# Weights converted in pieces of 1024 columns, a third query buffer and fewer filling products in a kernel of attention and a two-layer network

## The chip, the cores and the metric

The kernel runs on one core of a Trainium2 chip. The metric is the device time of one execution in microseconds. Before the change three runs gave 907.27, 908.99 and 909.57, a median of 908.99.

A core has five engines with a queue of instructions each, taken in order: TensorE (PE; its weight loads are shown as PEld), VectorE (DVE), ScalarE (ACT), GpSimd (POOL) and SyncE (SP), which here issues nearly all transfers. Sixteen DMA engines carry them out.

## The reference, cut to what matters

Attention of 8 batches, 8 heads, 576 positions and head dimension 64, within a window (heads 0 to 3: the last 32 positions; heads 4 to 7: every fourth of the last 128), then a two-layer network over 4608 tokens with d_model 512 and d_ff 2048:

```python
scores = scale * np.matmul(q, k.transpose(0, 1, 3, 2))
scores = np.where(masks[None], scores, -1000000000.0)
attn = np.exp(scores - np.max(scores, axis=-1, keepdims=True))
attn = attn / (np.sum(attn, axis=-1, keepdims=True) + 1e-09)
x = np.matmul(attn, v)          # then heads side by side: 4608 x 512
...
h = x @ w_in
sp = np.maximum(h, 0.0) + np.log1p(np.exp(-np.abs(h)))
g = h * erf(sp)
return (g @ w_out).astype(np.float32)
```

The two weight matrices arrive as numbers of 64 bits; the kernel turns each into a pair of 32-bit parts on the chip.

## The kernel before, in words

**Attention.** The work is cut into 72 units of 4 blocks of 64 queries. `scores` (32 small products, L214), `mask_max` on DVE (L225, four calls), `exponents` on ACT (L235, four calls), `normalize` (a reciprocal on DVE, a product on POOL, L247 and L248), `transposes` on PE (L253), `turned`, which copies their result out (L257), `values` (32 small products, L272), and `rows` on ACT (L314), which gathers the results as rows of x^T. When all units of a pair of heads are there, `finish` splits the row tile into a high and a low part (`part_hi` on ACT, L319; `part_lo` on DVE, L325), for the first tokens, or stores it (`store_x`, L344).

**The opening.** The first `FIRST` = 14 units are visited by `first_visit(n)`, with no large product beside them: visit n does the scores of unit n and the values of unit n - 3 (`LAG`), with `busy` filling products (L354) in between, on PE. Query tiles `qkz` are two, used in turn; `load_qk(n + 2)` follows the scores of n in SP's queue. Eight filling products stand ahead of the first visit; visits 0 to 2 have 6 each, the later ones 2 and 2. Visits 1 to 9 (`EARLY`) also convert weights, and copy the transposed probabilities by ACT; the others by DVE.

**The weights.** `prep` is a list of 32 pieces of 128 x 512 numbers (16 of w_in, 16 of w_out), sorted by the step that needs them. A piece is loaded by `load_w` (L421) into one of three places `dbl0` to `dbl2` of 512 KB. `prep_act` does two things on ACT: it copies a finished piece as the high part (L436), and takes the absolute value of the next loaded piece (L441). `prep_dve` subtracts for an earlier piece's low part (L450), and for the current one does a shift (L454) and two merges of bit fields (L455, L456); then the place is free and the next load into it is issued. One call handles each of three pieces at a different stage, one call per visit and afterwards one per half-step x. Intermediate values lie in a tile `w` with four buffers.

**The main loop.** x counts half-steps; step t = x // 2 handles 256 of the 2048 columns of d_ff for a chunk of 512 tokens, and x takes 128 of them. `mm1` (L518, 12 products; from the fourth chunk on `mm1_fast`, L639) fills the PSUM tile `h`; `take` (L660) copies it out by DVE and frees it; `argument` (Softplus, L664) and `table` (Erf, L667) are ACT's, `gate` (L674, L677, L678) is DVE's, `mm2` (L692, 12 products) runs two steps later. Units of attention are put in by `visits()`: one in each of x = 0 to 6, then at 9, 11 and 14, then two at a time by the list `PACE`. `weights(x)` stands ahead of `mm1` for x < 4, and behind the gate after that. `exponents` follow at even x. The order is written by hand, and each engine's queue has the order of the code.

**The saved sums.** The first chunk is done half, then the second whole, then the rest of the first. At x = 11 (`SAVED`) `save` copies the four partial sums out of PSUM and stores them: two go to the halves of `dbl2`, one to a tile of its own, one to `pz[1]`. Loads asked for at x = 11 are held until those stores are issued, and place 2 is not reloaded in x = 8 to 11; `load_w(2)` comes directly behind `save`. Later `dbl0` to `dbl2`, the tile `plain` and `w` serve other things: sums of weights (`sum_whole`, L528), fetched tokens, differences (`right_less`) and outputs (`store`).

Of the kernel before, what the change touches and what calls it, by code (L numbers as in the profile page):

```python
# [13 lines left out]
I32 = mybir.dt.int32  # L14
# [53 lines left out]
EARLY = 9  # L68
# [68 lines left out]
def attn_moe_kernel(ctx: ExitStack, tc: tile.TileContext, qk, v, masks, eye, w_in, w_out, out):  # L137
# [70 lines left out]
    def scores(u):  # L208
        i = u % 2
        for s in range(SPU):  # L210
            at, (p, r) = QW + key_start(u, s), divmod(s, SIDE)
            for h in range(2):
                hs = slice(h * D, (h + 1) * D)
                nc.tensor.matmul(sps[h][r * STRIP:(r + 1) * STRIP, i, p, :], qkz[i][hs, s * STRIP:(s + 1) * STRIP],  # L214
                                 qkz[i][hs, at:at + KEYS], start=True, stop=True,
# [133 lines left out]
    idle = plain.bitcast(BF16)[:, 0:TOK]  # L349
# [48 lines left out]

    def doubles(i):
        return io.tile([P, TOK, 2], I32, name=f"dbl{i}", bufs=1)  # L400
# [16 lines left out]
    def load_w(i):  # L417
        if prep:
            _, src, hi, lo = prep.pop(0)
            d = doubles(i)  # L420
# [3 lines left out]
    def like(w, part):  # L424

        return w.rearrange("p (a j n) -> p a j n", a=2, j=PAIR) if len(part.shape) == 4 else w

    calls = [0]

    def prep_act():  # L430


        calls[0] += 1
        if made:
            w, hi, lo = made.popleft()
            nc.scalar.copy(out=hi, in_=like(w, hi))  # L436
            rest.append((calls[0], w, hi, lo))
        if staged:
            i, d, hi, lo = staged.popleft()
            w = io.tile([P, TOK], F32, name="w", bufs=4)  # L440
            nc.scalar.activation(out=w, in_=d[:, :, 1].bitcast(F32), func=AF.Abs, scale=REBASE)  # L441
# [481 lines left out]
```

## Time and profile before

| | |
|---|---|
| Median of three runs | 908.99 us |
| Profiled execution, and its span | 909.89 us, 907.8 us |
| PE, PEld busy in the span | 886.3 us (98%), 754.2 us (83%) |
| DVE, ACT, POOL busy | 669.4 us (74%), 600.5 us (66%), 76.9 us (8%) |
| DMA moved | 188.89 MB, mean 208 GB/s |
| First product of the large matrices | 50.81 us |

The page gives busy times of the engines over the span, and groups of instructions by line. Views of the trace give the same for stretches of time, the waits (who waited for whom), the chain of work that ended last, and the instructions in order of time. An instruction's row has its start and its duration in microseconds, engine, line, operation, the tile written and the tiles read, the shape, and in brackets how long the engine had been idle and what released it. `dbl` is the place of a loaded piece, `w` its intermediate value, `win`, `wout_hi` and `wout_lo` the converted weights. A product counts as busy until its last result is out, so that consecutive ones overlap.

### The profile page before, as it was taken

The numbers are of one execution on the slowest core, as the hardware profiler recorded it, in microseconds if no ns is written. First come the engines' busy times: TensorE is split into PE (matmuls) and PEld (weight loads), VectorE is DVE, ScalarE is ACT, GpSimd is POOL, SyncE is SP. The second block draws the span as 40 slices with busy tenths as digits, with TensorE's granted clock in tenths as the row PEclk, the third lists the DMA queues.
The fourth block names the chain that finished last, engine by engine and source line by source line (L and its number), as shares of the span: only waits on it lengthen the run. The fifth ranks groups of instructions, "written<-read, shape, count | busy, mean of one in ns | idle before, by whom it ended". The sixth has DMA issues, their size and how long they took to land.

```text
span 907.8 us, 22886 instructions
## 1 busy us (share of the span) xinstructions
PE 886.3 (98%) x9142; PEld 754.2 (83%) x9142; DVE 669.4 (74%) x1703; ACT 600.5 (66%) x1266; POOL 76.9 (8%) x97
## 2 busy tenths in 40 slices
PE   7799999999999999999999999999999999999998
PEld 3467777888887888889988988888988999999996
DVE  5888878876788888667876777678666866776555
ACT  6889879876678687666776676669654644545442
POOL 2312100000011100000100000001000000000000
PEclk9899999999999999999999999999999999999999
DMA  8874444432459688777658765877566546656521
GB/s 276 278 258 151 123 164 130 155 109 94 156 190 330 216 304 296 245 274 233 217 212 284 264 211 189 290 262 256 179 242 230 181 149 230 235 176 205 200 82 47
DMA packets 69450, 188.89 MB, mean 208 GB/s; under 512 B 9184, under 2 KB 17632, under 8 KB 63200
## 3 DMA queue, kind: packets, MB, share of 16 engines
q1 hardware_dynamic: 69056, 186.91, 60.5%
q8 instruction: 72, 1.18, 0.5%
q10 hardware_dynamic: 288, 0.52, 0.1%
q14 instruction: 34, 0.28, 0.1%
HBM read 153.85 MB, written 33.55 MB: 206 GB/s over the span
## 4 chain that ended last, share of the span: by engine, by line
PE 85%; DVE 7%; ACT 3%; DMA 3%; issue 1%; POOL 0%; SPq 0%; DVEq 0%; POOLq 0%; ACTq 0%
PE acc L692 40%; PE h L639 15%; PE tx L639 12%; PE h L518 10%; PE sp L272 3%; PE sp L214 3%; DMA dbl<-in_w_in_dram 2%; PE sp L253 1%; ACT prob L235 1%; PE h L354 1%; DVE s L674 1%; DVE hc L660 1%; PE acc L272 1%; DVE ghi L677 0%; DVE w L455 0%
## 5 line engine op out<-in xcount | busy, mean ns | idle before, releaser
L692 PE MATMUL acc<-wout_hi,ghi 128*128 128x512 f32 x576 | 228.4, 397 | 0.4 <-DVE ghi L677 0.2
L692 PE MATMUL acc<-wout_lo,ghi 128*128 128x512 f32 x576 | 225.6, 392 | 0.0
L664 ACT ACTIVATE s<-hc 128x1024 f32<-128x1024 f32 x72 | 76.5, 1062 | 188.5 <-DVE hc L653 171.1
L692 PE MATMUL acc<-wout_hi,glo 128*128 128x512 f32 x576 | 159.0, 389 | 0.0
L692 PEld LDWEIGHTS acc<-wout_hi,glo 128*128 128x128 f32 x576 | 108.1, 188 | 22.8
L692 PEld LDWEIGHTS acc<-wout_hi,ghi 128*128 128x128 f32 x576 | 108.5, 188 | 20.6 <-DVE ghi L677 0.8
L692 PEld LDWEIGHTS acc<-wout_lo,ghi 128*128 128x128 f32 x576 | 108.6, 189 | 19.6
L248 POOL TENSOR_TENSOR prob<-prob,rinv 128x256 f32<-128x256 f32 x72 | 69.2, 971 | 536.0 <-DVE ssum L246 313.7
L678 DVE TENSOR_TENSOR glo<-s,ghi 128x512 fp32r<-128x512 f32 x144 | 100.0, 694 | 5.5 <-PE acc L692 0.5
L235 ACT ACTIVATE prob<-prob,nmax 128x64 f32<-128x64 f32 x288 | 96.4, 339 | 8.3 <-DVE nmax L225 7.8
L674 DVE TENSOR_TENSOR s<-hc,s 128x1024 f32<-128x1024 f32 x72 | 92.9, 1290 | 9.1 <-ACT s L667 9.0
L639 PE MATMUL h<-win 128*128 128x256 f32 x720 | 98.1, 283 | 0.0
L518 PE MATMUL h<-x,win 128*128 128x512 f32 x384 | 96.6, 393 | 1.5 <-DVE hc L660 1.5
L664 ACT ACT_TABLE_LOAD x72 | 92.4, 1283 | 1.3
L667 ACT ACT_TABLE_LOAD x72 | 92.4, 1283 | 1.3
L639 PEld LDWEIGHTS h<-win 128*128 128x128 f32 x720 | 91.6, 192 | 0.0
L518 PEld LDWEIGHTS h<-x,win 128*128 128x128 f32 x384 | 71.2, 188 | 17.5 <-DVE hc L660 2.3
L667 ACT ACTIVATE s<-s 128x1024 f32<-128x1024 f32 x72 | 76.3, 1060 | 0.8
L677 DVE CAST ghi<-s 128x512 fp32r<-128x512 f32 x144 | 68.4, 475 | 3.1 <-PE acc L692 0.6
L225 DVE CUSTOM_DVE_ANT_0 prob<-sp,cst 128x64 f32<-128x64 f32 x288 | 45.3, 219 | 33.9 <-ACT rows L314 20.8
L314 ACT COPY rows<-sp 128x128 f32<-128x128 f32 (+7 forms) x167 | 27.9, 307 | 57.1 <-PE sp L214 54.9
L649 DVE TENSOR_TENSOR hc<-h,hc 128x512 f32<-128x512 f32 x48 | 33.2, 692 | 41.2 <-PE h L639 40.9
(108 smaller groups left out, 1259.4 us busy)
## 6 DMA issues: line engine op xcount, KB each, us to landing
win<-ws SPq DMA_DIRECT2D x48, 1024.0 KB, 5.8
win<-ws SPq DMA_DIRECT2D x48, 768.0 KB, 4.4
v<-in_v_dram SPq DMA_DIRECT2D x72, 256.0 KB, 4.3
qk<-in_qk_dram SPq DMA_DIRECT2D x48, 272.0 KB, 4.1
dbl<-in_w_in_dram SPq DMA_DIRECT2D x16, 512.0 KB, 4.8
dbl<-in_w_out_dram SPq DMA_DIRECT2D x16, 512.0 KB, 3.7
ws<-x SPq DMA_DIRECT2D x32, 256.0 KB, 4.2
qk<-in_qk_dram SPq DMA_DIRECT2D x24, 288.0 KB, 4.4
```

Of the source, the lines that this page charges most:

```text
L225: nc.vector.tensor_tensor_reduce(out=pr[:, g, :], in0=sps[h][:, u % 2, p, :], in1=mask[QUADS.index(kinds(u, p))], scale=-SCALE, scalar=BIG ...
L235: nc.scalar.activation(out=probs[u][:, j, :], in_=probs[u][:, j, :], func=AF.Exp, scale=-1.0, bias=nmax[:, j:j + 1], accum_out=sums[u][:, ...
L248: nc.gpsimd.tensor_tensor(probs[u], probs[u], rinv.broadcast_to([P, 2 * PARTS, KEYS]), op=ALU.mult)
L272: nc.tensor.matmul(xp[h * D:(h + 1) * D, qs], vt[ks, s, h, :], pt[ks, h * P + s * STRIP:h * P + (s + 1) * STRIP], start=True, stop=True, t ...
L518: nc.tensor.matmul(h, win_at[:, ftp, j, cc // 2, w, cc % 2, :], x[cc], start=(k == 0 and i == 0), stop=(k == CC - 1 and i == 2))
L639: nc.tensor.matmul((h, bank)[b][:, half * HN:(half + 1) * HN], w[:, k, wi, c, :], x[:, xi, c, :], start=(c == 0 and n == 0), stop=(c == 1 ...
L664: nc.scalar.activation(out=ls[t], in_=hs[t], func=AF.Softplus)
L667: nc.scalar.activation(out=ls[t], in_=ls[t], func=AF.Erf)
L674: nc.vector.tensor_tensor(out=e, in0=hc, in1=e, op=ALU.mult)
L677: nc.vector.tensor_copy(out=ghi, in_=e[:, j])
L678: nc.vector.tensor_tensor(out=glo, in0=e[:, j], in1=ghi.bitcast(F32), op=ALU.subtract)
L692: nc.tensor.matmul(acc[tt], g[:, tt * P:(tt + 1) * P], w[:, ft, :], start=(first and w is wout_hi and g is ghi), stop=(last and g is glo))
```

## The change

- A piece has 1024 columns instead of 512, so there are 16: 8 of w_in, each with two of the four row blocks of 128, and 8 of w_out, each with two row blocks. The host lays the weights out so that a piece has 8 KB in a row for each partition. There are two places, `big0` and `big1`, of 1024 KB each; `load_w` is called ahead of visits 0 and 2.
- A piece takes two calls. The even call does the absolute value of one piece (`prep_abs`, from `prep_late`) and the shift and merges of the piece begun before; the odd call does the copy and the subtraction. In the opening calls belong to visits 3, 4, 5, 6, 8, 9, 11 and 12, and visit 2 has a first absolute value alone. In the loop, `prep_act` (the copy) moves to the head of x, `prep_late` stays where `prep_act` was.
- Intermediate values lie in `ring`, one tile of two times 1024 columns, later of four times 512 (`single`), instead of `w` and `plain`. The filling products read `pz[1]` instead of `plain`.
- A third query buffer, the first buffer of `hc`, serves units below 12 in turn with the other two; loads are issued three units ahead.
- Filling products: 4 instead of 8 ahead of the first visit, 3 instead of 6 in visits 0 to 2.
- `save` uses the spare tile, `pz[1]` and two row tiles. Nothing is withheld from the places of the weights, and the load behind `save` is gone.

```diff
-EARLY = 9
+EARLY = 3, 4, 5, 6, 8, 9, 11, 12
+DEEP = 12
+WIDE = 2 * TOK
...
+    qkz.append(work.tile([P, PAIR, TOK], F32, name="hc").rearrange("p f n -> p (f n)")[:, 0:QW + KW])
+
+    def qk_of(u):
+        return qkz[u % 3 if u < DEEP else u % 2]
...
-    plain = one.tile([P, 2 * TOK], F32, name="plain")
+    ring = one.tile([P, 2 * WIDE], F32, name="ring")
...
-            nc.sync.dma_start(out=qkz[u % 2][:, 0:n], in_=qk[u, :, 0:n])
+            nc.sync.dma_start(out=qk_of(u)[:, 0:n], in_=qk[u, :, 0:n])
...
-    idle = plain.bitcast(BF16)[:, 0:TOK]
+    idle = pz[1].bitcast(BF16)[:, 0:TOK]
...
-        copy = nc.scalar.copy if 1 <= n <= EARLY else nc.vector.tensor_copy
+        copy = nc.scalar.copy if n in EARLY else nc.vector.tensor_copy
         if has(m):
             transposes(m)
         scores(n)
-        load_qk(n + 2)
-        busy(2 if has(m) else 6)
+        if n != DEEP - 1:
+            load_qk(n + 3 if n < DEEP - 1 else n + 2)
+        busy(2 if has(m) else 3)
         if has(m):
             turned(m, copy)
-        if 1 <= n <= EARLY:
+        if n == 2:
+            prep_abs()
+        elif n in EARLY:
             prep_act()
+            prep_late()
...
-        for c in range(CC):
-            hi, lo = (win_at[:, 2 * g:2 * g + 2, :, c // 2, i, c % 2, :] for i in range(2))
-            prep.append((USED[2 * g], w_in[c, g], hi, lo))
-    for f in range(FT):
-        prep.append((2 + USED[f // PAIR], w_out[f], wout_hi[:, f, :], wout_lo[:, f, :]))
+        for k in range(2):
+            hi, lo = (win_at[:, 2 * g:2 * g + 2, :, k, i].rearrange("p a j c n -> p (a j) (c n)") for i in range(2))
+            prep.append((USED[2 * g], w_in[k, g], hi, lo))
+    for p in range(SPC):
+        hi, lo = (w[:, PAIR * p:PAIR * (p + 1), :] for w in (wout_hi, wout_lo))
+        prep.append((2 + USED[p], w_out[p], hi, lo))
...
+    def big(i):
+        return io.tile([P, 2 * WIDE], I32, name=f"big{i}", bufs=1)
+    later = {}
+    def part_of(i):
+        if i // 2 not in later:
+            later[i // 2] = big(i // 2)
+        return later[i // 2][:, i % 2 * WIDE:(i % 2 + 1) * WIDE]
     def doubles(i):
-        return io.tile([P, TOK, 2], I32, name=f"dbl{i}", bufs=1)
+        return part_of(i).rearrange("p (n w) -> p n w", w=2)
+    turns = [0, 0]
+    def single():
+        turns[0] += 1
+        return ring[:, (turns[0] - 1) % 4 * TOK:((turns[0] - 1) % 4 + 1) * TOK]
...
+    def prep_abs():
+        if staged:
+            i, d, hi, lo = staged.popleft()
+            w = ring[:, turns[1] % 2 * WIDE:(turns[1] % 2 + 1) * WIDE]
+            turns[1] += 1
+            nc.scalar.activation(out=w, in_=d[:, :, 1].bitcast(F32), func=AF.Abs, scale=REBASE)
+            begun.append((i, d, hi, lo, w))
     def prep_act():
-        calls[0] += 1
-        if made:
+        if calls[0] % 2 and made:
             w, hi, lo = made.popleft()
             nc.scalar.copy(out=hi, in_=like(w, hi))
-            rest.append((calls[0], w, hi, lo))
-        if staged:
-            i, d, hi, lo = staged.popleft()
-            w = io.tile([P, TOK], F32, name="w", bufs=4)
-            nc.scalar.activation(out=w, in_=d[:, :, 1].bitcast(F32), func=AF.Abs, scale=REBASE)
-            begun.append((calls[0], i, d, hi, lo, w))
+            rest.append((w, hi, lo))
+    def prep_late():
+        if calls[0] % 2 == 0:
+            prep_abs()
-    def prep_dve(keep=None):
-        if rest and rest[0][0] < calls[0]:
-            _, w, hi, lo = rest.popleft()
-            nc.vector.tensor_tensor(lo, like(w, lo), hi.bitcast(F32), op=ALU.subtract)
-        if begun and begun[0][0] < calls[0]:
-            _, i, d, hi, lo, w = begun.popleft()
+    def prep_dve():
+        if calls[0] % 2:
+            if rest:
+                w, hi, lo = rest.popleft()
+                nc.vector.tensor_tensor(lo, like(w, lo), hi.bitcast(F32), op=ALU.subtract)
+        elif begun:
+            i, d, hi, lo, w = begun.popleft()
             t = w.bitcast(I32)
             nc.vector.tensor_scalar(t, t, 3, None, op0=ALU.logical_shift_left)
             nc.vector.scalar_tensor_tensor(t, d[:, :, 1], -0x80000000, t, op0=ALU.bitwise_and, op1=ALU.bitwise_or)
             nc.vector.scalar_tensor_tensor(t, d[:, :, 0], 29, t, op0=ALU.logical_shift_right, op1=ALU.bitwise_or)
             made.append((w, hi, lo))
-            if i != keep:
-                soon(load_w, i)
+            soon(load_w, i)
+        calls[0] += 1
...
-        r = sums_of[p] = doubles(2).bitcast(F32).rearrange("p n w -> p (n w)") if p % 2 else plain
+        r = sums_of[p] = doubles(2).bitcast(F32).rearrange("p n w -> p (n w)") if p % 2 else part_of(3).bitcast(F32)
...
-            part = [o[:, 0:DM], o[:, DM:2 * DM], spare, pz[1]][tt]
+            part = (spare, pz[1])[tt] if tt < 2 else work.tile([P, S], F32, name="rows", bufs=4)[:, 0:DM]
...
-        busy(8)
+        busy(4)
         load_qk(0)
         nc.sync.dma_start(out=cst[:, 0:NMASK * KEYS], in_=masks)
         load_qk(1)
+        load_qk(2)
         nc.sync.dma_start(out=ident, in_=eye)
         for n in range(FIRST):
-            if n < 3:
-                load_w(n)
+            if n in (0, 2):
+                load_w(n // 2)
             first_visit(n)
-            if 1 <= n <= EARLY:
+            if n in EARLY:
                 prep_dve()
...
-                prep_act()
-                prep_dve(keep=2 if SAVED - 4 < x <= SAVED else None)
+                prep_late()
+                prep_dve()
...
+            if x not in pause:
+                prep_act()
             if t < 2:
                 turn(ready)
                 weights(x)
...
                     save()
                     hold(False)
-                    load_w(2)
```

More of the change, by code (lines that the diff above doesn't have):

```diff
@@ L208, in scores @@
     def scores(u):
-        i = u % 2
+        i, z = u % 2, qk_of(u)
         for s in range(SPU):
@@ L213, in scores @@
                 hs = slice(h * D, (h + 1) * D)
-                nc.tensor.matmul(sps[h][r * STRIP:(r + 1) * STRIP, i, p, :], qkz[i][hs, s * STRIP:(s + 1) * STRIP],
-                                 qkz[i][hs, at:at + KEYS], start=True, stop=True,
+                nc.tensor.matmul(sps[h][r * STRIP:(r + 1) * STRIP, i, p, :], z[hs, s * STRIP:(s + 1) * STRIP],
+                                 z[hs, at:at + KEYS], start=True, stop=True,
                                  tile_position=(h * D, r * STRIP))
@@ L419, in load_w @@
             _, src, hi, lo = prep.pop(0)
-            d = doubles(i)
+            d = big(i).rearrange("p (n w) -> p n w", w=2)
             nc.sync.dma_start(out=d, in_=src.bitcast(I32).rearrange("p (n w) -> p n w", w=2))
@@ L498, in fetch_x @@
                 hi, lo = (xs[cc][:, i, 0:TOK] for i in range(2))
-                src = io.tile([P, TOK], F32, name="w", bufs=4)
+                src = single()
             kept[cc] = hi, lo, src
@@ L601, in right_less @@
     def right_less(c, to, a, b):
-        w = wholes[to] = io.tile([P, TOK], F32, name="w", bufs=4)
+        w = wholes[to] = single()
         a, b = (wholes[n] if n in wholes else cells[c][n].bitcast(F32)[:, 1] for n in (a, b))
@@ L704, in save @@
     def save():
-        o = doubles(2).bitcast(F32).rearrange("p n w -> p (n w)")
         spare = small.tile([P, DM], F32, name="o", bufs=1)
         for tt in range(TOK // P):
-            part = [o[:, 0:DM], o[:, DM:2 * DM], spare, pz[1]][tt]
+            part = (spare, pz[1])[tt] if tt < 2 else work.tile([P, S], F32, name="rows", bufs=4)[:, 0:DM]
             copy_for(tt)(out=part, in_=acc[tt])
@@ L714, in fetch @@
         for tt in range(TOK // P):
-            o = io.tile([P, DM], F32, name="w", bufs=4)
+            o = single()
             nc.sync.dma_start(out=o, in_=partial[tt])
@@ L728, in store @@
                 else:
-                    o = io.tile([P, DM], F32, name="w", bufs=4)
+                    o = single()
                 copy_for(tt)(out=o, in_=acc[tt])
@@ L912 @@
         "eye": np.eye(P, dtype=np.float32),
-        "w_in": np.ascontiguousarray(w_in.reshape(CC, P, DF // TOK, TOK).transpose(0, 2, 1, 3)),
-        "w_out": np.ascontiguousarray(w_out.reshape(FT, P, DM)),
+        "w_in": np.ascontiguousarray(w_in.reshape(2, 2, P, DF // TOK, 2 * PAIR, P).transpose(0, 3, 2, 4, 1, 5)).reshape(2, DF // TOK, P, WIDE),
+        "w_out": np.ascontiguousarray(w_out.reshape(SPC, PAIR, P, DM).transpose(0, 2, 1, 3)).reshape(SPC, P, WIDE),
     }
```

2 lines of the change are left out of this document (1 added, 1 removed).

## The prediction

> **What bounds the kernel now.** I read the page's totals first, then busy time by stage, then the chain of waits, and last the queues of the stages that lose time. The stages are cut at starts of first-layer products: the attention-only opening ends at 50.81, the loop's steps x = 0 to 3 end at 69.24, 4 to 6 at 90.79, 7 to 11 at 121.37, 12 to 14 at 141.20.
>
> ```profile
> span 907.8 us, 22886 instructions
> ```
>
> ```profile
> 0.00:15.00 15.00, 11.69 (x194) 5.25 (x194) 5.52 (x39) 8.04 (x30) 2.61 (x10) 1.00 0.79 256
> 33.00:36.00 3.00, 2.38 (x36) 1.49 (x36) 2.74 (x6) 2.94 (x14) 1.63 (x2) 0.50 0.74 257
> 36.00:39.00 3.00, 3.00 (x68) 1.65 (x68) 2.18 (x11) 2.24 (x10) 0.83 (x2) 0.50 0.85 265
> 0.00:50.81 50.81, 38.80 (x895) 19.77 (x895) 33.35 (x163) 37.29 (x163) 14.01 (x30) 0.93 0.83 268
> 16.67:51.96 35.29, 28.13 (x705) 15.46 (x706) 27.51 (x124) 28.73 (x132) 11.40 (x20) 0.90 0.83 271
> 50.81:69.24 18.43, 16.73 (x313) 12.66 (x312) 16.78 (x54) 16.31 (x46) 2.57 (x4) 1.00 0.81 268
> 69.24:90.79 21.55, 21.18 (x271) 16.20 (x271) 19.08 (x58) 20.05 (x59) 5.03 (x7) 1.00 0.45 151
> 90.79:121.37 30.58, 30.45 (x263) 24.34 (x253) 26.87 (x63) 27.82 (x47) 5.89 (x6) 1.00 0.36 108
> 121.37:141.20 19.83, 18.41 (x148) 14.40 (x138) 15.72 (x37) 12.95 (x25) 0.61 (x1) 1.00 0.51 173
> 141.20:907.76 766.56, 760.72 (x7289) 666.78 (x7278) 557.57 (x1333) 486.04 (x929) 48.75 (x49) 1.00 0.61 209
> ```
>
> Columns: stretch, its length, busy time of PE, weight load, DVE, ACT and POOL, granted clock, DMA share, GB/s. From 141.20 on PE is busy 760.72 of 766.56 us and the change touches none of its work there, so little can be won or lost. What PE loses lies ahead of that: in the opening its 38.80 us are largely filling products, DMA is busy 0.83 of the time, and no product of the large matrices runs. The second place is 50.81 to 69.24, where PE idles 1.70 us and DVE is busy 16.78 of 18.43. The third is 121.37 to 141.20, with 1.42 us idle; 69.24 to 90.79 has 0.37.
>
> ```profile
> 6.00 5.37 DMA dbl<-in_w_in_dram
> 13.32 5.08 DMA dbl<-in_w_in_dram
> 23.68 6.67 DMA dbl<-in_w_in_dram
> ...
> 126.37 4.91 DMA dbl<-in_w_in_dram
> ```
>
> In the chain of waits (start, length, what) the weight loads are the only long pieces that are not PE: three in the opening and one at 126.37, which belongs to the buffer that the saved partial sums had occupied.
>
> ```profile
> 14.45 0.68 ACT L441 ACTIVATE w<-dbl 128x512 f32<-128x512 f32 x1 [0.28 <-DMA dbl<-in_w_in_dram]
> ...
> 131.36 0.67 ACT L441 ACTIVATE w<-dbl 128x512 f32<-128x512 f32 x1 [4.08 <-DMA dbl<-in_w_in_dram]
> ```
>
> The last row shows the damage: ACT takes its queue in order, so the absolute value of a weight piece held 4.08 us of it, and the error function behind it came that much later.
>
> **The opening, part by part.** ACT is the engine to follow, since every visit's exponents stand in its queue behind that visit's weight work. Exponents of visit 3 end at 16.67 and those of visit 13 at 51.96, hence the fifth row above. Within it:
>
> ```profile
> L441 ACT ACTIVATE w<-dbl 128x512 f32<-128x512 f32 x6 | 4.1, 691 | 2.4 <-DMA dbl<-in_w_in_dram 2.4
> L436 ACT CAST win<-w 128x512 fp32r<-128x512 f32 x6 | 3.8, 633 | 0.6 <-DVE w L456 0.6
> ...
> L257 ACT COPY pT<-acc 128x256 f32<-128x256 f32 x6 | 2.3, 376 | 0.0
> ```
>
> ```profile
> ACT rows L314 <- PE acc L272: 3.4, 4, 1.2
> ```
>
> So of 35.29 us, 2.4 + 0.6 + 3.4 = 6.4 are waits, and the rest, 28.9, is work. The change alters that work little. It drops 6 absolute values and 6 copies of 512 columns, 6 x (0.69 + 0.63) = 7.9 us, and puts in 3 absolute values and 4 copies of 1024, for visits 4 to 13. No such call of 1024 is in the trace: it costs no more than two of 512 (1.38 and 1.27), and hardly less than ACT's nearest row:
>
> ```profile
> L664 ACT ACTIVATE s<-hc 128x1024 f32<-128x1024 f32 x72 | 76.5, 1062 | 188.5 <-DVE hc L653 171.1
> ```
>
> I take 1.06 for both, as they are the same engine and size: 7 x 1.06 = 7.4, and one more transposed copy falls to ACT (7 instead of 6, +0.38). Work: 28.9 - 7.9 + 7.4 + 0.4 = 28.8.
>
> The waits do change, and bytes decide them.
>
> ```profile
> dbl<-in_w_in_dram SPq DMA_DIRECT2D x8, 512.0 KB, 5.1
> v<-in_v_dram SPq DMA_DIRECT2D x12, 256.0 KB, 4.4
> qk<-in_qk_dram SPq DMA_DIRECT2D x10, 272.0 KB, 4.6
> ```
>
> A load becomes 1024 KB, there are two places for it instead of three, and the second is issued at the head of visit 2. Visit 3 needs it on ACT, ahead of its exponents. SP's queue has by then sent five query loads, one value load and both weight loads: 5 x 0.279 + 0.262 + 2 x 1.049 = 3.75 MB (masks and identity are small). At the 256 GB/s of the first 15 us that lands at 14.7. With DMA at 0.79 there is room, since a third query load and a large weight load queue up earlier: 256 / 0.79 = 324 GB/s would bring it at 11.6. I take 14. Before, the absolute value of visit 3 started at 14.45 and its exponents ended 2.2 us later; a call 0.4 longer ends them at 16.6. Nothing is won up to there: the 4 filling products fewer at the start, and the first exponents perhaps a microsecond earlier, are swallowed by this wait. If the load is late instead, all of it is lost in turn.
>
> After that: the third piece is loaded when DVE is through with the first, about 14, into the same place; with two visits' queries and values (2 x 0.54 MB) ahead of it, 2.1 MB at 271 GB/s take 7.9 and land at 21.9; ACT wants it one visit (28.8 / 10 = 2.9) and a transposed copy (0.4) after 16.6, at 19.9: wait 2.0. The following loads have three visits and none. Copies wait for DVE as before, 0.6. The waits of rows for PE, 3.4 in four visits without weight work, stay in three, 2.6. Sum 5.2 against 6.4. The opening ends (16.67 - 16.6) + (28.9 - 28.8) + (6.4 - 5.2) = 1.4 us sooner.
>
> The third query buffer takes away a wait which PE had, but not for its whole length:
>
> ```profile
> PE sp L214 <- DMA qk<-in_qk_dram: 4.5, 4, 1.6
> ```
>
> In those 4.5 us ACT was held by weight loads or had its own backlog, so I give it nothing alone; it is the cover under which the rest holds. It lives in a tile of the second layer's input that is first needed after visit 11, so it delays none. Bounds for the opening: with the load at 14.7 and calls of 1024 at two of 512 (7 x 0.26 = 1.8 more) it is 1.1 us later than before; with the load at 11.6 and no wait of the third piece it is 1.4 + 2.4 + 2.0 = 5.8 sooner.
>
> **Steps 0 to 3.** These have no second product; DVE sets the pace.
>
> ```profile
> L455 DVE SCALAR_TENSOR_TENSOR w<-dbl,w 128x512 int32<-128x512 int32 x32 | 22.2, 692 | 1.1
> ...
> L454 DVE TENSOR_SCALAR w<-w 128x512 int32<-128x512 int32 x32 | 13.9, 433 | 0.0
> ...
> L528 DVE TENSOR_TENSOR dbl<-win 128x1024 f32<-128x1024 f32 x4 | 4.9, 1217 | 0.0
> ```
>
> Two pieces of 512 cost DVE 2 x (0.43 + 3 x 0.69) = 5.0 (both merges and the subtraction taken at 0.69). One of 1024 costs 3 x 1.22 + 0.8 = 4.5; the shift has no row at 1024 and lies between 0.43 and 0.87. Four steps do two such pairs: 1.1 us less. The work now alternates, 3.2 on even steps and 1.2 on odd ones, where the gating product stands, so the queues fit better. PE's own need:
>
> ```profile
> 82.97 0.60 PE sp L272 x32
> 83.57 0.39 PE sp L214 x32
> 83.95 2.96 PE h L518 x12
> 86.91 0.22 PE sp L253 x2
> 87.13 2.75 PE acc L692 x12
> ```
>
> Without the last row a step is 4.17, four are 16.7 against 18.43: at most 1.7 to win. I take 1.2. The cover needed is that the piece loaded at step 0 lands before step 2.
>
> **Steps 4 to 11.** With the last row a step is 6.92; the three of 69.24 to 90.79 should take 20.8 instead of 21.55, and the lighter DVE and ACT queues should give 0.6 of that 0.8. Steps 7 to 11 have 0.13 us of idle PE: nothing.
>
> **The saved sums.** They go to a spare tile, a transposed-weights tile and two row tiles, no longer to a landing place of weights, and the late load after them goes. Row tiles two and three in turn were last read by step 8, three steps earlier. What is late next is the ordinary chain, with the piece loaded two steps ahead. Steps 12 to 14 need 3 x 6.92 less two units' 1.21 = 18.3 against 19.83, and PE idles 1.42: I take 1.4, from nothing to 1.5.
>
> **The rest.** Sums of weights use one more half of the weights' place instead of the old filler tile, and small buffers come from the ring, four in turn as before: zero, if different halves of a tile don't wait for each other; eight such waits of DVE for ACT at 1 us would cost little, PE being ahead only by its own queue.
>
> Sum: 1.4 + 1.2 + 0.6 + 1.4 = 4.6 us less. The profiled execution took 909.89 (span 907.8 and 2.1 around it); it would take 905.3. The three runs' median, 908.99, lies 0.9 lower, which gives 904.4.
>
> **Rivals.** *The opening isn't limited by bytes.* If a load's time is a fixed part and a slower growing one, the second piece is there when wanted, at about 12 instead of 14, and the third's wait of 2.0 goes too: 4.0 us more, 900.4. The DMA share of 0.83 speaks against it, its being 0.79 early speaks for it. The Trainium skill, "DMA: Bandwidth & Descriptors", section on the anatomy of one DMA, gives 2.0 us plus bytes over 436 GB/s, by which, as an estimate, 1024 KB take 4.4 us where two of 512 KB take 6.4 together; with the 5.1 us of this trace for 512 KB the rows disagree, as loads share the engines here.
>
> *The clock falls more.* From 33 to 39 the clock is at 0.50, after a stretch in which PE only waited in pieces. Fewer filling products and one longer wait before visit 3 may bring a second such 6 us; PE is busy 5.38 of them, and at full clock half of that, so up to 2.7 us more: 907.1. The Trainium skill, "TensorE: Matmul & The Clock Gate", Part 1, puts the fall after an idle window of about 3.4 us, which speaks against the removal of fillers; here it fell although PE's longest wait for queries was 1.6.
>
> *Slower: two places starve ACT.* Between DVE's last read of a place and ACT's next use lie two visits of (35.29 - 1.4) / 10 = 3.4 us for the third piece, three for each of the next three, two steps (8.6 us by 17.2 / 4) for the seventh. Landings of 11 us give waits of 4.2, 3 x 0.8 and 2.4, in all 9.0 against my 2.0: 911.4. From about 10.5 on they take the whole gain. For it: 512 KB took up to 6.67 while DMA was busy. Against it: the total of bytes hardly changes.
>
> *It does little:* queries were not the limit, waits only change place, 908.
>
> **Chances.** Forecast 0.45 (own range 901 to 906.5); not byte-limited 0.20; clock 0.20; starved 0.10; nothing 0.05. About 0.3%, 2.7 us, is what can be told from no change: faster means under 906.3. Forecast, the second case and a third of the clock's make 0.72; the rest of the clock's and the last 0.18; starved 0.10. The range from 897 to 909 leaves out the starved case and what lies below the opening's better bound.
>
> **What would show it.** Right: first large product near 49, the absolute value's wait in visit 3 around 2 to 3 us and one of 1 to 2 in visit 5, no wait near 131, steps 0 to 3 in about 17.2 us, 1024-column calls at 1.06 on ACT and 1.22 on DVE. Wrong: waits of ACT for weights in visits 8 and 11 or at step 2, half clock for more than 8 us after 15, a changed length of what follows the step after the saved sums.

## The result and the profile after

The changed kernel takes 917.56 us (median of four runs, 916.64 to 920.4) against 908.27 (four runs) for the kernel before on the same chip: ratio 1.0107, 95% interval 1.008 to 1.0133. It is slower; 904.4 had been predicted, in a range from 897 to 909. The profiled execution took 920.4.

The page's first line, and busy time by stage as it was shown of before (cut at the same products):

```profile
span 918.6 us, 22694 instructions
```

```profile
0.00:55.98 55.98, 40.30 (x869) 21.64 (x882) 31.89 (x148) 38.22 (x161) 16.33 (x30) 0.80 0.73 249
55.98:79.93 23.95, 20.09 (x312) 15.51 (x310) 16.33 (x47) 16.05 (x42) 3.39 (x4) 0.82 0.71 236
79.93:101.14 21.21, 21.05 (x281) 16.20 (x271) 18.61 (x51) 19.81 (x54) 4.01 (x7) 1.00 0.40 132
101.14:131.29 30.15, 30.15 (x263) 24.42 (x252) 23.73 (x53) 24.18 (x40) 4.21 (x6) 1.00 0.39 134
131.29:150.72 19.43, 18.10 (x149) 14.38 (x139) 16.37 (x32) 15.31 (x24) 0.61 (x1) 1.00 0.44 154
150.72:918.55 767.83, 761.09 (x7289) 666.45 (x7278) 552.82 (x1310) 483.06 (x919) 46.93 (x49) 1.00 0.61 208
```

Read it against the rows of before: the opening is 55.98 instead of 50.81, steps 0 to 3 are 23.95 instead of 18.43, both at a mean clock of about 0.8 where it had been 0.93 and 1.00, and both with less DMA (0.73 and 0.71 for 0.83 and 0.81). So the sixteen DMA engines as a whole were less loaded than before in both. Steps 4 to 11 won 0.8, steps 12 to 14 only 0.4, and the long rest lost 1.3. The same kernel profiled a second time (*a_again* below) took 918.0, its median, with 54.67 and 22.82 in the first two stages and the others as here. I use it to divide up the loss: opening +3.9, steps 0 to 3 +4.4, steps 4 to 14 -1.2, steps 15 to 22 +1.5, together 8.6; its span is 8.4 longer, so from step 23 on nothing is lost.

The chain of waits (start, length, what) has changed its transfers: before, three weight loads of the opening; now one weight load, one query load and two loads of values.

```profile
1.63 4.33 DMA qk<-in_qk_dram
7.75 7.73 DMA big<-in_w_in_dram
37.94 6.33 DMA v<-in_v_dram
56.33 3.56 PE h L552 x12
62.80 9.05 DMA v<-in_v_dram
```

The last one is the largest single wait. SP's issues around it, and what PE says of it:

```profile
60.28 0.33 SPq L450 DMA_DIRECT2D big<-in_w_out_dram  x1
60.66 1.28 SPq L819 DMA_DIRECT2D x<-x  x2
62.04 0.71 SPq L206 DMA_DIRECT2D qk<-in_qk_dram  x1
62.80 0.48 SPq L210 DMA_DIRECT2D v<-in_v_dram  x1
```

```profile
51.66 0.69 PE L261 MATMUL acc<-ident,prob 128*128 128x128 f32 x2 [1.97 <-POOL prob L256]
...
71.98 1.08 PE L280 MATMUL acc<-pT,v 64*64 64x32 f32 x32 [3.86 <-DMA v<-in_v_dram]
```

A weight load of 1024 KB, two stores and a query load are issued ahead of 256 KB of values, which land 9.05 us after their issue; PE stands still for 3.86 us in step 2. The weight load itself stood in SP's queue until DVE had freed its place, and what is behind it waited along: the two stores went out at 60.66, and at 55.28 in *a_vloop* below, where the weight load comes later. In *a_again* PE waits 4.2 us at the same place; the other late load of values in the chain is not in that profile, whose opening has no wait of PE for values at all.

The next pair of views is ACT and DVE in the opening's last visits:

```profile
45.52 0.62 ACT L322 COPY rows<-acc 128x112 f32<-128x112 f32 x3 [1.92 <-PE acc L280]
46.17 0.67 ACT L327 CAST x<-rows 128x576 fp32r<-128x576 f32 x1
...
50.78 1.05 ACT L471 CAST win<-ring 128x1024 fp32r<-128x1024 f32 x1 [2.35 <-DVE ring L490]
```

```profile
46.87 0.76 DVE L333 TENSOR_TENSOR x<-rows,x 128x576 fp32r<-128x576 f32 x1 [3.54 <-ACT x L327]
47.55 0.69 DVE L488 TENSOR_SCALAR ring<-ring 128x1024 int32<-128x1024 int32 x1
48.27 1.23 DVE L489 SCALAR_TENSOR_TENSOR ring<-big,ring 128x1024 int32<-128x1024 int32 x1
49.53 1.22 DVE L490 SCALAR_TENSOR_TENSOR ring<-big,ring 128x1024 int32<-128x1024 int32 x1
50.67 0.17 DVE L255 RECIPROCAL rinv<-ssum 128x4 f32<-128x4 f32 x1
```

PE's values of that visit had themselves waited for a late load (issued at 37.94, in the chain above). ACT gathers the rows late, DVE's split of the row tile waits 3.54 for ACT, and only then does DVE reach the piece of weights: 3.2 us without a gap, with the next unit's reciprocal behind it. In the kernel before, visits 10 to 13 had no conversion. ACT's copy waits 2.35 for the last merge, and PE's transposes 1.97 for POOL, which waits for the reciprocal. *a_again* has both waits too, 2.36 and 1.97.

The third place is behind step 12: ACT, then DVE.

```profile
165.56 1.05 ACT L471 CAST wout_hi<-ring 128x1024 fp32r<-128x1024 f32 x1 [2.24 <-DVE ring L490]
166.63 1.28 ACT L701 ACT_TABLE_LOAD   x1
167.92 1.06 ACT L701 ACTIVATE s<-s 128x1024 f32<-128x1024 f32 x1
```

```profile
169.01 1.23 DVE L708 TENSOR_TENSOR s<-hc,s 128x1024 f32<-128x1024 f32 x1 [2.53 <-ACT s L701]
```

The weight copy now stands at the head of the half-step. It waits 2.24 us for DVE's merges, and the error function and its table load stand behind it, so the gating product comes 2.53 us late.

Terms that can be read off directly, ACT's absolute value of the second piece and one row of a group for each 1024-column call (count, then busy time and mean ns):

```profile
15.51 1.14 ACT L463 ACTIVATE ring<-big 128x1024 f32<-128x1024 f32 x1 [3.40 <-DMA big<-in_w_in_dram]
```

```profile
L463 ACT ACTIVATE ring<-big 128x1024 f32<-128x1024 f32 x16 | 18.4, 1148 | 4.4 <-DMA big<-in_w_in_dram 4.2
L471 ACT CAST win<-ring 128x1024 fp32r<-128x1024 f32 x8 | 8.4, 1052 | 10.0 <-DVE ring L490 10.0
L490 DVE SCALAR_TENSOR_TENSOR ring<-big,ring 128x1024 int32<-128x1024 int32 x16 | 20.8, 1298 | 0.6
```

### The profile page after: what moved, and what is told of

It is laid out like the page before. It is cut to its first block, busy times and chain, and to the rows that moved or that the text cites. A ratio compares the mean times of both kernels' runs of the same rounds, so it can differ in the third digit from the quotient of the medians.

```text
span 918.6 us, 22694 instructions
## 1 busy us (share of the span) xinstructions
PE 890.8 (97%) x9117; PEld 758.6 (83%) x9129; DVE 659.8 (72%) x1638; ACT 596.6 (65%) x1234; POOL 75.5 (8%) x97
## 4 chain that ended last, share of the span: by engine, by line
PE 78%; DVE 10%; ACT 5%; DMA 3%; issue 2%; POOL 1%; SPq 0%; DVEq 0%; POOLq 0%; ACTq 0%
PE acc L726 36%; PE h L673 15%; PE tx L673 12%; PE h L552 7%; PE sp L280 3%; PE sp L222 2%; DMA v<-in_v_dram 2%; DVE s L708 1%; ACT L701 1%; PE sp L261 1%; DVE ring L489 1%; DVE ring L490 1%; ACT s L701 1%; DVE ghi L711 1%; DVE hc L694 1%
## 5 line engine op out<-in xcount | busy, mean ns | idle before, releaser
L256 POOL TENSOR_TENSOR prob<-prob,rinv 128x256 f32<-128x256 f32 x72 | 66.6, 936 | 546.9 <-DVE ssum L254 316.4
L552 PE MATMUL h<-x,win 128*128 128x512 f32 x384 | 99.5, 403 | 0.7 <-DVE hc L694 0.7
L552 PEld LDWEIGHTS h<-x,win 128*128 128x128 f32 x384 | 73.5, 194 | 17.1 <-DVE hc L694 1.1
```

The lines of the kernel that those rows point to most:

```text
L256: nc.gpsimd.tensor_tensor(probs[u], probs[u], rinv.broadcast_to([P, 2 * PARTS, KEYS]), op=ALU.mult)
L552: nc.tensor.matmul(h, win_at[:, ftp, j, cc // 2, w, cc % 2, :], x[cc], start=(k == 0 and i == 0), stop=(k == CC - 1 and i == 2))
```

## The experiments

**Theory:** three queues kept in order now hold up urgent work behind weight work: SP's transfers (small loads behind 1024 KB), DVE's block of 3.2 us in the last visits, ACT's copy ahead of the error function. **Rivals:** the filling products that were taken out (the clock), and the new places of the saved sums or the third query buffer being dearer than they look. Names with *a_* are edits of the changed kernel, those with *b_* of the kernel before. Ratios are to the kernel before on the same chip, with 95% intervals; stage lengths are of the profiled execution.

**Loads of values ahead of weights.** *a_vfirst* issues the weight loads of visits 8 and 11 and of the main loop behind the query and value loads of that visit or half-step; *a_vloop* does so in the main loop alone:

```
     def prep_dve():
...
-            soon(load_w, i)
+            late.append(i)
...
                 soon(load_v, n - 1)
+            flush()                           # soon(load_w, i) for each i in late
```

> The changed kernel, with the weight loads that are asked for in visits 8 and 11 and in the main loop put behind the next query and value loads of SP's queue. Theory (bytes ahead of value loads): the value load of step 0 lands before step 2 needs it, the wait of 3.9 us at values there goes, the one of 1.3 in visit 11 too, and with them their followers; steps 0 to 3 take 18 to 20 us instead of 23.9, the opening 1 to 3 us less; 910 to 913. Rival (the clock and missing filling products): the value waits only hide what the half clock costs, the time stays within 2 us of 917.5. Rival (ACT and DVE queues): the stages keep their length, and the waits are put down to ACT instead, 915 to 917.

> The changed kernel with the weight loads put behind the next query and value loads in the main loop only, the opening as it was. With that edit in both places step 2 fell from 8.8 to 6.0 us and steps 0 to 3 from 23.9 to 20.2, but the time did not fall. Theory (bytes ahead of value loads, and the opening's own loads hurt by the same edit): steps 0 to 3 take 20 us, the opening 54.5 to 56, 913 to 915. Rival (what is won in step 2 is lost later): the later stages are longer by 3 us, 917 to 918.

*a_vfirst*: 919.84, ratio 1.0121 (1.0101 to 1.0142). *a_vloop*: 917.87, 1.0105 (1.0088 to 1.0122). The wait of step 2 goes, as SP and PE of *a_vloop* show:

```profile
61.19 0.38 SPq L210 DMA_DIRECT2D v<-in_v_dram  x1
61.62 0.42 SPq L456 DMA_DIRECT2D big<-in_w_out_dram  x1
```

```profile
67.82 0.67 PE L280 MATMUL acc<-pT,v 64*64 64x32 f32 x32
68.42 0.45 PE L222 MATMUL sp<-qk 64*32 64x64 f32 x32
...
70.70 0.44 PE L261 MATMUL acc<-ident,prob 128*128 128x128 f32 x2 [1.83 <-POOL prob L256]
```

Step 2 falls from 8.84 (8.50 in *a_again*) to 6.02 and steps 0 to 3 from 22.8 to 20.5. The time of the kernel does not show it: neither ratio is below the changed kernel's beyond the intervals. Part of the 2.8 us is taken up by what was hidden behind the wait, the same block of DVE as in the opening: it starts at 65.77, a copy follows, the reciprocal ends at 69.87, and PE waits 1.83 for the product of POOL. In *a_vfirst* the opening is also longer, 57.02, than in any other profile. So the late values are shown as a wait, and not as a share of the 9.3 us.

**Conversions away from the last visits.** *a_early* makes six calls in the opening instead of eight, *a_early2* makes all eight, one visit sooner at the end:

```
-EARLY = 3, 4, 5, 6, 8, 9, 11, 12
+EARLY = 3, 4, 5, 6, 8, 9             # a_early
+EARLY = 3, 4, 5, 6, 8, 9, 10, 11     # a_early2
```

> The changed kernel with conversions only in visits 3, 4, 5, 6, 8 and 9, so that the conversion of visit 11, which stands on DVE behind the split of the fourth row tile, moves to step 0 (the copies of transposed probabilities in visits 11 and 12 go to DVE with it). Theory (DVE conversion in the way of the next visit's reciprocal and maxima): the wait of PE for probabilities of 2.0 us before visit 13 and that of ACT for DVE of 2.4 in visit 12 go, the opening is 3 to 5 us shorter, what comes after no longer than 1 us more; 913 to 915. Rival (bytes only): the value load of visit 11 still sits behind a weight load, the opening loses at most 1 us; 916 to 918.

> The changed kernel with conversions in visits 3, 4, 5, 6, 8, 9, 10 and 11 instead of 3, 4, 5, 6, 8, 9, 11 and 12: as many calls, but the last merges stand in visit 10 and not behind the split of the fourth row tile in visit 11. With two calls fewer the opening ended at 50.1, and the second matrix's weights came too late at steps 20 to 26 by 8 us of PE waits. Theory: the opening ends at 50 to 53 and nothing is late afterwards, 911 to 915. Rival (the opening's length comes from how much is converted in it, not from where): 54 to 57, 916 to 919.

*a_early*: 926.62, 1.0195 (1.0179 to 1.0211), slower still. *a_early2*: 916.43, 1.0088 (1.0072 to 1.0103). The opening of *a_early* ends at 50.11, where the kernel before had 50.81: without the calls of visits 11 and 12, and the load that they issue, the opening's loss is gone in this profile. But one piece fewer at the start makes all later ones late. PE's waits from 190 on:

```profile
PE acc L726 <- DVE wout_lo L484: 5.0, 3, 2.5
PE acc L726 <- ACT wout_hi L471: 3.2, 1, 3.2
```

In all, what follows step 23 is 11 us longer, which no kernel here without this edit shows: the conversion of the second matrix has no slack. *a_early2* keeps the schedule, ends its opening at 53.03, and wins 1.1 to 1.6 us of median. But *a_mix2* below makes the same calls in the same opening, and its profile ends it at 55.0: 53.03 cannot be put down to the visits.

**The copy behind the error function.** *a_erf* moves ACT's weight copy back, from half-step 4 on, behind the error function:

```
-            if x not in pause:
+            if x not in pause and t < 2:
                 prep_act()
...
                 table(t - 1)
+            if x not in pause and t >= 2:
+                prep_act()
```

> The changed kernel with the copy of a converted piece on ACT behind the error function of its half-step instead of at the head, from x = 4 on. Theory (copy ahead of the error function): ACT no longer waits for DVE's merges before it does the error function, DVE's wait of 2.2 to 2.5 us for it goes in odd steps from 11 on, and the steps at x = 12, 18 and 22 lose 1.2, 0.9 and 0.5 us; 914.5 to 915.5, nothing changed ahead of x = 4. Rival: DVE's total, not the order, sets these steps; within 0.7 us of 917.5.

915.12, 1.0065 (1.0043 to 1.0087): 2.4 us less than the changed kernel. Its steps 12 to 14, its ACT, and DVE's longest waits from 100 to 200, first in the changed kernel and then here:

```profile
130.04:147.83 17.79, 17.79 (x150) 14.47 (x139) 16.18 (x31) 12.23 (x19) 1.41 (x1) 1.00 0.43 150
```

```profile
159.30 1.06 ACT L701 ACTIVATE s<-s 128x1024 f32<-128x1024 f32 x1
...
161.24 1.05 ACT L471 CAST wout_hi<-ring 128x1024 fp32r<-128x1024 f32 x1 [0.87 <-DVE ring L490]
```

```profile
DVE s L708 <- ACT s L701: 16.7, 8, 2.5
```

```profile
DVE hc L694 <- PE h L552: 13.6, 13, 3.7
```

DVE no longer waits for the error function but for PE, which is the bound again: busy 17.79 of 17.79 us. Steps 12 to 14 go from 19.43 to 17.79 and 15 to 22 from 47.77 to 46.21. The four kernels below that have this edit, too, take 64.0 to 64.2 us for steps 12 to 22, where the changed kernel takes 67.2.

**The saved sums alone.** *b_save* gives the kernel before the new places and drops the late load:

```
-            part = [o[:, 0:DM], o[:, DM:2 * DM], spare, pz[1]][tt]
+            part = (spare, pz[1])[tt] if tt < 2 else work.tile([P, S], F32, name="rows", bufs=4)[:, 0:DM]
...
-                prep_dve(keep=2 if SAVED - 4 < x <= SAVED else None)
+                prep_dve()
...
-                    load_w(2)
```

> The kernel before with the new places of the saved sums alone: no place of the weights is withheld and no load stands behind the stores. Prediction's term: 1.4 us less in steps 12 to 14, nothing elsewhere; 907 against 908.3. Rival: the other steps take it back, no difference.

906.53, 0.9969 (0.9956 to 0.9982), 2.15 us faster: the fastest of all versions here, and faster than both kernels. Steps 12 to 14, 19.83 before:

```profile
121.63:139.87 18.24, 18.09 (x149) 14.38 (x139) 17.16 (x39) 12.62 (x24) 1.41 (x1) 1.00 0.51 175
```

So this part of the change works, and in the changed kernel the moved copy took its gain.

**The third query buffer alone**, and with the saved sums (*b_query3*, *b_both*; the buffer as in the change):

```
+    qkz.append(work.tile([P, PAIR, TOK], F32, name="hc").rearrange("p f n -> p (f n)")[:, 0:QW + KW])
...
-        load_qk(n + 2)
+        if n != DEEP - 1:
+            load_qk(n + 3 if n < DEEP - 1 else n + 2)
```

> The kernel before with the third query buffer alone. Prediction: PE's waits for queries (4.5 us) go, ACT's backlog keeps the opening's length, 0 to 1 us less. Rival (bytes ahead of others): query loads issued earlier push the weight and value loads back, 0 to 2 us more. Rival: the query waits were on the path, 2 to 4 us less.

> The kernel before with the new places of the saved sums and the third query buffer, pieces of 512 columns as before. The two alone gave 2.2 and 0.8 us less; they act in different stages, so 905 to 906.3 together. Rival: the earlier query loads only shift the opening's waits, as the interval of that run reaches 1.0, 906.5 to 907.

907.9, 0.9987 (0.9973 to 1.0001), and 906.8, 0.9985 (0.9973 to 0.9996). Alone its median is 0.8 us lower, and the interval takes in no change; a gain over the saved sums alone doesn't show: the profile of *b_both* has its first large product at 48.31 and is the shortest of all (span 903.9), but its median is not below *b_save*'s.

**Filling products.** *a_fillers* puts the old number back, *b_fillers* takes them from the kernel before; *a_warm* and *b_warm* put 4 and 4 into the later visits instead of 2 and 2:

```
-        busy(4)                          # a_fillers; b_fillers the other way
+        busy(8)
-        busy(2 if has(m) else 3)
+        busy(2 if has(m) else 6)
...
-        busy(2 if has(m) else 3)         # a_warm; b_warm likewise, with 6
+        busy(4 if has(m) else 3)
...
             values(m)
-            busy(2)
+            busy(4)
```

> The changed kernel with the filling products of before (8 at the start, 6 in visits 0 to 2). Theory of the loads: the first visits are up to 1 us later, which the wait for the second weight piece in visit 3 swallows; the half clock comes as often, since it follows from PE's later waits; 916.5 to 918.5. Rival (the clock): half clock for one stretch at most, as before, and 3 us or more less; 912 to 914.5.

> The kernel before with the fewer filling products alone. Prediction: nothing, as the loads decide, within 0.7 us of 908.3. Rival (the clock): more half clock in the opening, 1.5 to 4 us more.

> The changed kernel with 4 and 4 filling products instead of 2 and 2 in every visit from 3 on. If the half clock of PE makes the opening long, the clock stays at full speed in most of it and the opening ends 2 to 4 us sooner, 914 to 915.5. If PE is only waiting for the others there, the opening keeps its length or grows by 1 to 3 us, since a visit gets 0.9 us of products more, 917 to 920.

> The kernel before with 4 and 4 filling products instead of 2 and 2 in every visit from 3 on, the control for the run with the same edit of the changed kernel. PE's visit grows by 0.9 us, of which ACT's and DVE's queues hide most: 908 to 911; if the one stretch at half clock mattered, 906 to 908.

*a_fillers* 918.47, 1.0097 (1.0075 to 1.012); *b_fillers* 908.46, 1.0000 (0.9987 to 1.0014): the fillers taken out at the start cost nothing that can be told. *a_warm* 914.5, 1.0070 (1.0053 to 1.0088); *b_warm* 909.32, 1.0012 (1.0002 to 1.0022). More fillers later win 3.5 us over *a_again* in the changed kernel and lose 1.0 in the kernel before. From 15 to 30 the changed kernel and *a_warm* had (clock: third column from the right)

```profile
15.00:30.00 15.00, 11.82 (x247) 6.20 (x249) 9.96 (x45) 12.30 (x49) 4.83 (x8) 0.61 0.81 280
```

```profile
15.00:30.00 15.00, 12.60 (x296) 6.91 (x294) 10.82 (x45) 12.24 (x49) 3.85 (x9) 0.99 0.83 280
```

*a_fillers*, with the old number at the start, has 0.66 in that stretch, so the lower clock doesn't come from the edit of the fillers. Whether it is a cause of its own isn't shown. For it speaks the gain of *a_warm*, and that *a_again*'s two executions at 0.979 and 0.981 took 921.4 to 921.7 where those at 0.985 to 0.988 took 917.3 to 918.0; but longer waits could bring both. Against it: *b_fillers* had 0.80 from 15 to 30, where the kernel before had 1.00, and lost nothing, and *a_all* below, at 1.00 from 0 to 56, took 912.01, where its expectation put 909.5 to 911 for a cause of its own and 912 to 914 for fillers that only make the values of step 2 less late. Nor does the fall behind step 2 cost much: the twelve products of step 3 take 4.49 us in *a_all* and 3.00 at full clock in *a_two*, the whole step 5.41 and 5.16.

**Together.** *a_again* is the changed kernel unedited. *a_three* has the edits of *a_vfirst*, *a_early* and *a_erf*; *a_two* those of *a_vloop* and *a_erf*; *a_mix2* those of *a_vloop*, *a_early2* and *a_erf*; *a_all* those of *a_mix2* and *a_warm*.

> The changed kernel once more, unedited, on the chip of the next three. Its profiled execution lay 2.8 us above its own median, and edits that shorten steps 0 to 3 by 3.4 us in the profile left the median where it was. Either the timed executions are shorter in the opening than the profiled one (then this profile has its first large product at 53 to 54 and its steps 0 to 3 near 24 us), or in steps 0 to 3 (then those are near 20.5 us here and the value wait of step 2 comes and goes). Time 916.5 to 918.5.

> The changed kernel with three edits together: weight loads behind the next query and value loads (visit 8 and main loop), conversions only in visits 3, 4, 5, 6, 8 and 9, the copy behind the error function from x = 4 on. If the three causes are the loss and are separate, their gains add up: 904 to 908, at or under the kernel before. If one mechanism lies behind all of it, the sum is no more than the best of the three: 911 or above.

> The changed kernel with weight loads behind the next query and value loads in the main loop and the copy on ACT behind the error function from x = 4; conversions in the visits of the changed kernel. With the visits 3, 4, 5, 6, 8, 9, 10 and 11 as well it took 913.2, with an opening of 55.0 in the profile, where those visits alone had 53.0. If the place of the conversions in the opening matters, this is slower than that, 914.5 to 916; if not, it is the same, 912.5 to 914.

> The changed kernel with three edits: conversions in visits 3, 4, 5, 6, 8, 9, 10 and 11; weight loads behind the next query and value loads in the main loop; the copy on ACT behind the error function from x = 4. If the three causes are separate their gains add: 4 + 3.5 + 2.5 us under 917.5, 906 to 909. If one of them only moves the loss, 910 to 914.

> The changed kernel with four edits: conversions in visits 3, 4, 5, 6, 8, 9, 10 and 11; weight loads behind the next query and value loads in the main loop; the copy on ACT behind the error function from x = 4; 4 and 4 filling products in every visit from 3 on. The first three took 913.2, the fourth alone gave 3.3 us less. If the half clock is a cause of its own, 909.5 to 911; if the filling products only made the value load of step 2 less late, which the second edit has done already, 912 to 914.

| | median, us | ratio (95%) | opening ends | steps 0-3 | 12-22 |
|---|---|---|---|---|---|
| a_again | 918.0 | 1.0119 (1.0097 to 1.0142) | 54.67 | 22.82 | 67.21 |
| a_three | 923.46 | 1.0156 (1.0125 to 1.0187) | 50.21 | 20.45 | 64.22 |
| a_two | 914.63 | 1.0067 (1.005 to 1.0084) | 55.38 | 20.09 | 63.99 |
| a_mix2 | 913.18 | 1.0047 (1.0033 to 1.0061) | 55.0 | 21.03 | 63.99 |
| a_all | 912.01 | 1.0033 (1.002 to 1.0046) | 53.31 | 20.42 | 64.0 |
| before | | | 50.81 | 18.43 | 66.07 |

*a_three* suffers from *a_early*'s late pieces (what follows step 23 is again longer, by some 14 us). The others bring the loss from 9.3 to 3.0 us; *a_all*'s lead over *a_mix2* is within their intervals. *a_mix2* had been expected at 906 to 909 if the gains of its three edits add up as the stages showed them, 10 us. What adds up is the gains in the medians: nothing, 1.1 and 2.4 make 3.5, and *a_mix2* is 4.4 below the changed kernel. What is left of *a_all*'s profile stands at the same places: opening +2.5, steps 0 to 3 +2.0, against -2.1 in steps 12 to 22 and -0.8 in steps 4 to 11. In its opening the second piece still holds ACT:

```profile
15.54 1.12 ACT L469 ACTIVATE ring<-big 128x1024 f32<-128x1024 f32 x1 [3.62 <-DMA big<-in_w_in_dram]
```

Visit 3's exponents, behind it in ACT's queue, end at 18.20 there and ended at 16.67 in the kernel before: 1.5 of the 2.5 us.

## Why the prediction was wrong

**"The opening ends ... 1.4 us sooner": failed, +3.9 to +5.2.** Counted as the forecast counted, by ACT's exponents (the changed kernel, then *a_again*), those of visit 13 end 4.7 and 3.4 us later than before. The sum's three terms: up to visit 3, "nothing is won up to there" was a loss of 1.5, since the second piece was there at 15.5 in both, neither at 14 nor by the late bound of 14.7, and the exponents ended at 18.18 instead of 16.6. ACT's work held: the calls cost 1.05 and 1.15 (1.06), and all of it 29.5 and 29.2 us for the 28.8 foreseen. ACT's waits were mis-sized, 8.9 and 7.9 for 5.2, although the third piece's wait of 2.0 came as nothing and 0.3. "Copies wait for DVE as before, 0.6" became 2.5 and 2.4: the shift and merges ahead of the copy are now one block of 0.69 + 1.23 + 1.22 = 3.1 us where they had been 0.43 + 2 x 0.69 = 1.8, and one such block stands in visit 11, where there had been none. "The waits of rows for PE ... stay in three, 2.6" became 6.4 and 4.9. One of them, 1.92, stands behind values that came late. I had counted bytes for the weights' own landing, and never for what is queued behind them. But *a_again* has its 4.9 without a late value, so most of this term has another cause, which stays open; it is 2.2 in *a_warm* and 4.9 in *a_all*, both at full clock.

Without the calls of visits 11 and 12 *a_early* and *a_three* end the opening at 50.11 and 50.21, so those calls carry the loss. As that edit also takes 2.9 us of work off ACT (an absolute value, a copy, two transposed copies), it doesn't tell their place from their amount. *a_early2* and *a_mix2*, with the same amount one visit sooner, end at 53.03 and 55.0 and don't settle it. Nor is settled how far late values matter, as *a_vfirst*, which puts them first at visits 8 and 11, did not shorten the opening.

**"Steps 0 to 3 ... in about 17.2": failed, 22.8 to 23.9.** I named as cover only "that the piece loaded at step 0 lands before step 2"; it does, ACT doesn't wait for it there. The step that failed was "so the queues fit better". The even step's block of 3.2 us stands ahead of the reciprocal, and the freed place's load ahead of the values. *a_vloop* shows the second wait and, once it is gone, the trace shows the first; no run moved the reciprocal ahead of the block, so that part is read and not tested.

**"Steps 4 to 11": right in sign,** 0.35 and 0.4 won for 0.6.

**"The saved sums ... 1.4": mechanism right, and the cover missed.** Alone it is 2.15 us of median, and 1.6 in steps 12 to 14. "What is late next is the ordinary chain" was wrong in this change: I listed the moved copy in the change and gave it no cost on ACT's queue, of which I had just quoted how an absolute value ahead of the error function had cost 4.08. It costs 2.4 to 2.9 us in the medians (*a_erf* against the two medians of the changed kernel), and 1.64 + 1.56 = 3.2 in the two stages.

**"From 141.20 on ... the change touches none of its work there": wrong.** Four pieces of 1024 columns are still copied between there and step 22, and there the moved copy lost 1.5.

**Rivals.** *Not byte-limited*: the DMA share fell to 0.73, yet the time did not. *The clock falls more*: it did, for 9 us at a stretch where 6 had been foreseen, but the premise, fewer fillers, is refuted by *a_fillers* and *b_fillers*; what the clock cost isn't settled, between 3.5 us (*a_warm*) and the 1.2 of *a_all* over *a_mix2*, which is within the intervals. *Two places starve ACT*: behind visit 3 ACT's waits for landings in the opening were 0 and 0.3; the kernel was slower all the same, and in step 2 it was PE that stood still, 3.86 us, for values behind the large load. *Third query buffer nothing*: held.

**What stays open.** Mending the late values shortens steps 0 to 3 by 1.8 to 3.9 us against the two profiles of the changed kernel, and the median hardly: *a_two* is 0.5 below *a_erf*, *a_vloop* level with the changed kernel. One profile shows one execution, and openings of the same code up to there differ by 1.3 us (54.67 to 55.98), those of *a_early2* and *a_mix2* by 2.0, so part of it may be scatter and part is given back to POOL and to the block. And of the 2.5 us that remain in *a_all*'s opening, 1.5 lie ahead of visit 4, behind the wait of 3.62; a smaller first load was not tried.

## What to carry to other kernels

Merging two calls into one, and two loads into one, saves little work but lengthens the stretch for which a queue cannot be interrupted, here on DVE from 1.8 to 3.1 us; for each urgent small item (a load, a reciprocal, an activation) look up what stands ahead of it in its queue after the change. Where a step moves ahead of another on an engine, price the wait that it brings with it, not its own duration. And a part of a change that is good by itself should be timed by itself: here the new places for four tiles were worth 2.15 us, and nothing of it was to be seen in the whole.

## What the hardware showed that I had not expected

**A product of POOL slows beside DVE.** One operation, the first while DVE merges 1024 columns, the second while DVE is at the maxima:

```profile
34.27 1.57 POOL L256 TENSOR_TENSOR prob<-prob,rinv 128x256 f32<-128x256 f32 x1
...
37.16 0.61 POOL L256 TENSOR_TENSOR prob<-prob,rinv 128x256 f32<-128x256 f32 x1 [0.16 <-DVE nmax L233]
```

The Trainium skill, "GPSIMD Engine Reference", section 1, says that the two share their memory interfaces and contend when a DVE instruction has two inputs there. The trace agrees, and gives the price: 1.0 us on POOL, in whose product the transposes of the next unit have their start.

**The clock falls without a long idle.** From 21 to 30 the changed kernel ran at 0.50, and PE's longest wait between 15 and 31 was 1.47 us. The Trainium skill, "TensorE: Matmul & The Clock Gate", Part 1, puts the fall after an idle window of about 3.4 us. If that means one wait of this length, the traces here don't agree; what kept the clock up from 15 to 30 was a denser row of fillers (*a_warm*, 0.99).

**1024 KB take 6.3 us**, the median of the four loads of the first matrix in the opening, and what is issued behind them 6.33 and 9.05, where 256 KB had taken 4.4 in the median. Over the whole run the medians are 5.2 for the first matrix and 4.8 for the second. By the figures of the Trainium skill, "DMA: Bandwidth & Descriptors", section on the anatomy of one DMA, 1024 KB issued by GpSimd would take an estimated 4.4. The loads here, issued by SP while the engines were busy 0.73 of the time, took longer; how much of it the sharing makes wasn't separated.
